# Half of each batch's attention attended a phase later, one stage a slot, with the first loads and weights asked for in another order

## The chip, the cores and the metric

The kernel runs on one core of a Trainium2 chip. A core has five engines that run beside each other, each with its own instruction stream: TensorE (PE in the profile; its weight loads are PEld), VectorE (DVE), ScalarE (ACT), GpSimd (POOL) and SyncE (SP, which here only starts DMAs). DMAs that SP starts and DMAs that GpSimd starts stand in different queues of the same 16 DMA engines. The metric is the device time of one execution in microseconds (us); the kernel before took 290.09 us, the median of three runs.

## The reference

Attention over a sliding window of 128 keys with 4 always visible first keys ("sinks"), followed by a gated feed-forward network (FFN). Everything comes in and goes out in float32.

```python
# q, k, v: (4, 8, 768, 64) = batch, heads, positions, head size
scores = matmul(q, k.T) / sqrt(64)
keep = (key < 4) | ((0 <= query - key) & (query - key < 128))
a = softmax(where(keep, scores, -1e9))
attn = matmul(a, v)                                  # (4, 8, 768, 64)
x = attn.transpose(0, 2, 1, 3).reshape(3072, 512)    # heads side by side
out = (maximum(x @ w_gate, 0) * (x @ w_val)) @ w_out # w: 512x1536, 512x1536, 1536x512
```

## The kernel before

**Units.** Two heads of one batch make a unit; there are 16 units, 4 to a batch, U[0] to U[15]. A unit goes through stages, each a function:

- `load_kq` (lines 91 to 93) and `load_v` (95 to 104) start its DMAs on SP: two for keys and queries into `kf` and `qf` (three buffers each), six for values into `vf` (four buffers).
- `cast_kq` (115) and `cast_v` (109, 111) turn them into bf16 on GpSimd: `kn` and `qn` (two buffers each), `vn` (four).
- `T` (line 179) transposes keys and queries on TensorE, 48 small matmuls, and ScalarE copies them out as `kE` and `qT`. In the head (while `head[0]` is true) the query copy is VectorE's.
- `Sg(u, g)` (197 to 207), shortened to S: the scores of group g (0, 1 or 2), on TensorE, and their exp on ScalarE. The band mask is added by two more matmuls (line 197, `bias=True`) for batch 0, and multiplied in by VectorE (line 207) for the others.
- `V(u, part)` (218 to 228): values and row sums of one half of the unit's 768 positions, on TensorE, then four VectorE operations that divide and write into `xT`. Half 0 needs S of groups 0 and 1, half 1 of groups 1 and 2.

**The FFN.** `chunk(b, g, m)` (lines 240 to 247) computes column block m (128 of the 1536 hidden columns, 12 blocks) of half g of batch b: four matmuls with `wg`, four with `wv`, a relu on ScalarE, a product on VectorE. It needs half g of all four units of batch b. `ffn2` (260 to 265) is one matmul with `w_out`; after twelve of them ScalarE copies a block of the output and SP stores it.

**Weights.** `load_w(m0, m1)` (line 123) starts two DMAs on GpSimd's queue, for column blocks m0 to m1 of `wg` and `wv`; `load_wo` (127) does so for a third of `w_out`. These DMAs turn float32 into bf16 on their way.

**Order.** The program is written under a manual schedule: each engine executes its instructions in the order of the text. A head prepares units 0 to 3 and attends the first half of each. Then follow 96 slots, one chunk each; behind the chunk stand the stages that `plan` has put into the slot, and then up to three queued `ffn2` calls (there are some from slot 24 on). Slots 0 to 23 belong to batch 0's FFN, and batch 1 is attended in them: 30 stages, of which the first six go one to a slot and the other 24 into slots 6 to 23 (`plan[6 + x * 18 // 24]`). All of batch 1, both halves, is attended in the first 24 slots, all of batch 2 in the next 24, and so on. From slot 24 on there is one stage a slot, up to slot 71. `pre` puts a unit's preparation, `front`, four slots ahead of its `T`: casts of keys, queries and values, and then the loads of the unit after it.

`gate(u)` (line 119) writes two elements of the key buffer from GpSimd. The load of that buffer, on SP, must wait for this write, and so cannot start before GpSimd has come to this place in its order.

The lines in the profile are those of this listing.

Of the kernel before, what the change touches and what calls it, by code (L numbers as in the profile page):

```python
# [19 lines left out]
def kernel(  # L20
# [12 lines left out]
    nc = tc.nc  # L33
# [54 lines left out]

    U = [Unit(i) for i in range(B * NP)]

    def load_kq(u):
        for x, dst in ((k, kf[u.i % NQ]), (q, qf[u.i % NQ])):
            nc.sync.dma_start(out=dst[:], in_=x[u.b, 2 * u.p:2 * u.p + 2].rearrange("h (p n) d -> (h p) (n d)", n=NR))

    def load_v(u):

# [16 lines left out]
    def cast_kq(u):  # L113
        for src, dst in ((kf[u.i % NQ], kn[u.i % 2]), (qf[u.i % NQ], qn[u.i % 2])):
            nc.gpsimd.tensor_copy(dst[:], src[:])  # L115
# [151 lines left out]
    with tc.manual_schedule():  # L267
        for i in range(NV):
            nc.vector.memset(vf[i][:, 6, :, :], 0.0)
        for i, what in ((0, load_kq), (1, load_kq), (2, load_kq), (0, load_v)):  # L270
            what(U[i])
        setup()
        gp_copy, ve_copy = nc.gpsimd.tensor_copy, nc.vector.tensor_copy
        cast_kq(U[0])
        T(U[0])
        cast_kq(U[1])
        T(U[1])
        load_kq(U[3])
# [32 lines left out]
        def prep(i):  # L311
            cast_kq(U[i])
            cast_v(U[i], gp_copy)

        def load(i):
            if i < len(U):
                load_kq(U[i])
                load_v(U[i])

        def front(i):  # L320

            prep(i)
            if i == 4:
                gate(U[5])
                load(5)
                load_w(8, 12)
            elif i == 5:
                gate(U[6])
                load(6)
# [5 lines left out]
        f2 = deque()  # L335
        slots = [(0, 0, m) for m in range(6)] + [(0, 1, m) for m in range(6)]
        slots += [(0, g, m) for m in range(6, FM) for g in range(2)]
        for b in range(1, B):
            slots += [(b, g, m) for g in range(2) for m in range(FM)]
        plan = [[] for _ in slots]  # L340
        first = [("V", 0, 1), ("S", 2, 2), ("V", 1, 1), ("S", 3, 2), ("V", 2, 1), ("V", 3, 1)]
        for s, x in enumerate(first):
            plan[s].append(x)
        later = [("T", NP, 0)]
        for i in range(NP, len(U)):
            later.append(("S", i, 0))
            if i > NP:
                later.append(("V", i - 1, 1))
            later.append(("S", i, 1))
            if i + 1 < len(U):  # L350
                later.append(("T", i + 1, 0))
            later += [("V", i, 0), ("S", i, 2)]
        later.append(("V", len(U) - 1, 1))
        for x, st in enumerate(later):
            plan[6 + x * 18 // 24 if x < 24 else x].append(st)
        pre = [[] for _ in slots]
        for s, p in enumerate(plan):
            for st in p:
                if st[0] == "T":
                    pre[max(0, s - 4)].append(st[1])  # L360
        for s, (b, g, m) in enumerate(slots):
# [55 lines left out]
```

## Time and profile before

| | |
|---|---|
| three runs | 290.72, 290.09, 287.62 us; median 290.09 |
| profiled execution | 290.54 us, of which its span (first to last instruction) is 288.8 |
| TensorE busy | 264.0 us, 91% of the span |
| VectorE, ScalarE, GpSimd busy | 146.0, 131.3, 59.9 us |
| read from memory | 28.48 MB, 120 GB/s over the span |
| mean granted TensorE clock | 0.969 of full speed |

The profile is of one execution. Times count from the span's start. A row of the timeline has start and length in us, the engine, the line of the kernel, the operation, output and inputs by their names with shapes, and in brackets the idle time before it and what ended it; neighbouring instructions of one line are merged (x8). A small q behind an engine's name (SPq) is its instruction queue, where DMAs are started. TensorE can be given a lower clock for a time; the granted clock says what share of full speed it had. Matmuls are pipelined and their ends are modelled, so start to start of neighbouring rows is a better measure than a row's length.

### The profile page before, as it was taken

To read this page: it belongs to the slowest core of one execution; us is meant where nothing else is said; L and a number is where in the kernel's file an instruction comes from. 1 tells how busy PE (TensorE), PEld (TensorE's weight loads), DVE (VectorE), ACT (ScalarE), POOL (GpSimd) and SP (SyncE) were. 2 spreads that over 40 slices of the span, in tenths; PEclk is the share of its full clock that TensorE was granted. 3 is DMA by queue.
4 is the path that set the end of the run, shared out by engine and by line. 5 is a ranking of instruction groups with operands and counts; after the bars stand their busy time and mean duration, and the time that the engine had idled before them with its cause. 6 is when DMAs were issued, how large, how long until landed. Compare 5 with 4: busy or idle time off the path is not lost.

```text
span 288.8 us, 6483 instructions
## 1 busy us (share of the span) xinstructions
PE 264.0 (91%) x2648; PEld 146.0 (51%) x2648; DVE 146.0 (51%) x287; ACT 131.3 (45%) x262; POOL 59.9 (21%) x87
## 2 busy tenths in 40 slices
PE   2983699598998999999999999999999999999994
PEld 1441365355555455555555555555555555555441
DVE  5373357348778655656564646565567322332100
ACT  3581123564675645464545464654543223233221
POOL 7661551614641302240042104000000000000000
PEclk9997589889999999999999999999999999999999
DMA  7999879599970006430346006010000010010122
GB/s 245 289 161 238 141 156 203 103 221 237 299 193 2 0 2 201 132 75 36 96 125 186 36 7 198 36 39 2 36 37 2 37 39 36 36 39 36 72 79 104
DMA packets 40557, 30.46 MB, mean 105 GB/s; under 512 B 27728, under 2 KB 33360, under 8 KB 40528
## 3 DMA queue, kind: packets, MB, share of 16 engines
q1 hardware_dynamic: 34720, 25.34, 29.7%
q0 software_dynamic: 5808, 4.72, 10.9%
q8 instruction: 20, 0.33, 0.5%
q14 instruction: 9, 0.07, 0.1%
HBM read 28.48 MB, written 6.29 MB: 120 GB/s over the span
## 4 chain that ended last, share of the span: by engine, by line
PE 79%; DVE 8%; DMA 5%; ACT 3%; SPq 2%; issue 1%; POOL 1%; ACTq 0%
PE g L240 20%; PE g L260 20%; PE g L245 20%; PE pp L218 6%; PE pp L201 4%; PE pp L260 4%; PE pp L179 3%; DMA vf<-in_v_dram 3%; DVE R L226 2%; DMA qf<-in_q_dram 2%; DVE t L224 2%; DVE xT L228 1%; PE pp L197 1%; SPq L98 1%; ACT qT L187 1%
## 5 line engine op out<-in xcount | busy, mean ns | idle before, releaser
L247 DVE TENSOR_TENSOR hT<-gs,g 128x384 bf16<-128x384 f32 x96 | 53.0, 552 | 77.4 <-PE g L245 50.9
L243 ACT ACTIVATE gs<-g 128x384 f32<-128x384 f32 x96 | 47.7, 496 | 78.0 <-PE g L240 77.2
L240 PE MATMUL g<-xT,wg 128*128 128x384 bf16 x384 | 80.3, 332 | 3.0 <-DVE xT L228 3.0
L245 PE MATMUL g<-xT,wv 128*128 128x384 bf16 x384 | 79.5, 331 | 0.0
L260 PE MATMUL g<-wo,hT 128*128 128x512 bf16 x240 | 64.4, 382 | 0.0
L205 ACT ACTIVATE ee<-pp 128x998 bf16<-128x998 f32 (+2 forms) x48 | 46.0, 966 | 34.2 <-PE pp L201 34.0
L240 PEld LDWEIGHTS <-wg 128*128 128x128 bf16 x384 | 35.9, 98 | 33.2 <-issue 2.9
L245 PEld LDWEIGHTS <-wv 128*128 128x128 bf16 x384 | 37.9, 99 | 28.2 <-issue 4.0
L260 PEld LDWEIGHTS <-hT 128*128 128x128 bf16 x288 | 24.2, 98 | 25.2 <-issue 3.3
L207 DVE TENSOR_TENSOR ee<-ee,msk 128x998 bf16<-128x998 bf16 (+2 forms) x36 | 24.9, 691 | 22.2 <-ACT ee L205 22.2
L115 POOL CAST kn<-kf 128x768 bf16<-128x768 f32 x16 | 14.1, 878 | 75.2 <-DMA kf<-in_k_dram 65.6
L201 PE MATMUL pp<-qT,kE 64*128 64x255 bf16 (+4 forms) x224 | 19.0, 262 | 3.9 <-DVE xT L228 2.0
L109 POOL CAST vn<-vf 128x896 bf16<-128x896 f32 x16 | 15.1, 946 | 35.5 <-DMA vf<-in_v_dram 26.8
L218 PEld LDWEIGHTS <-vn 128*64 128x64 bf16 x288 | 12.8, 113 | 17.9 <-issue 9.3
L264 ACT COPY ot<-g 128x512 f32<-128x512 f32 x20 | 11.9, 594 | 17.4 <-PE g L260 17.4
L226 DVE STREAM_TRANSPOSE R<-r 128x384 f32<-128x384 f32 x32 | 18.5, 578 | 1.1
L201 PEld LDWEIGHTS <-kE 64*128 64x128 bf16 x224 | 7.4, 96 | 21.1 <-issue 17.9
L224 DVE STREAM_TRANSPOSE t<-pp 128x384 f32<-128x384 f32 x28 | 16.2, 580 | 3.5 <-PE pp L218 3.2
L228 DVE TENSOR_TENSOR xT<-pp,R 128x384 bf16<-128x384 f32 x28 | 15.6, 557 | 1.0
L115 POOL CAST qn<-qf 128x768 bf16<-128x768 f32 x16 | 13.6, 853 | 8.3 <-DMA qf<-in_q_dram 8.2
L218 PE MATMUL pp<-ee,vn 128*64 128x255 bf16 (+8 forms) x256 | 14.8, 242 | 0.0
L218 PE MATMUL pp<-ee,ones 128*64 128x255 bf16 (+8 forms) x256 | 14.0, 237 | 0.0
(54 smaller groups left out, 151.0 us busy)
## 6 DMA issues: line engine op xcount, KB each, us to landing
kf<-in_k_dram SPq DMA_DIRECT2D x16, 384.0 KB, 3.3
qf<-in_q_dram SPq DMA_DIRECT2D x16, 384.0 KB, 4.2
out_dram<-ot SPq DMA_DIRECT2D x24, 256.0 KB, 2.0
vf<-in_v_dram SPq DMA_DIRECT2D x48, 64.0 KB, 4.5
vf<-in_v_dram SPq DMA_DIRECT2D x32, 96.0 KB, 3.6
wo<-in_moe_w_out_dram POOLq DMA_DIRECT2D x3, 512.0 KB, 10.5
wg<-in_moe_w_gate_dram POOLq DMA_DIRECT2D x2, 512.0 KB, 6.5
wv<-in_moe_w_val_dram POOLq DMA_DIRECT2D x2, 512.0 KB, 8.7
```

What stands on the lines that cost most here:

```text
L115: nc.gpsimd.tensor_copy(dst[:], src[:])
L201: nc.tensor.matmul(out=ps[:, h, c0:c1], lhsT=kE[t][64 * h:64 * h + 64, x0:x0 + 128], rhs=qT[t][64 * h:64 * h + 64, q0:q0 + c1 - c0], start ...
L205: nc.scalar.activation(x, ps[:, :, 0:n], Act.Exp, bias=0.0, scale=scale)
L207: nc.vector.tensor_tensor(x, x, msk[:, g, 0:n].unsqueeze(1).to_broadcast([128, 2, n]), op=Alu.mult)
L218: nc.tensor.matmul(out=(pv, pd)[which][64 * h:64 * h + 64, o0:o0 + c1 - c0], lhsT=w, rhs=ee[u.i % NE][:, g, h, c0:c1], start=i == 0, stop= ...
L224: nc.vector.transpose(out=t1[:], in_=pd[:, 0:CUT])
L226: nc.vector.transpose(out=R[:].rearrange("p (c e) -> p c e", e=32), in_=r[:].unsqueeze(2).to_broadcast([128, CUT // 32, 32]))
L240: nc.tensor.matmul(out=gp[:, 0:CUT], lhsT=wg[:, ko, m * 128:(m + 1) * 128], rhs=x[:, ko, c], start=ko == 0, stop=ko == KO - 1)
L243: nc.scalar.activation(gs[:], gp[:, 0:CUT], Act.Relu, bias=0.0, scale=1.0)
L245: nc.tensor.matmul(out=vp[:, 0:CUT], lhsT=wv[:, ko, m * 128:(m + 1) * 128], rhs=x[:, ko, c], start=ko == 0, stop=ko == KO - 1)
L247: nc.vector.tensor_tensor(h[:, m, c], gs[:], vp[:, 0:CUT], op=Alu.mult)
L260: nc.tensor.matmul(out=op, lhsT=hT[b % 2][:, m, t * 128:(t + 1) * 128], rhs=wo[:, m, :], start=m == 0, stop=m == FM - 1)
```

## The change

It has three parts. The first key and query loads (units 0 to 2) are started on ScalarE's queue instead of SP's. The first weights are asked for later in GpSimd's order: two column blocks at a time, the first behind unit 2's value cast, two more behind unit 3's, and two pairs at the end of the head, with unit 4's loads between them; unit 4's loads stood ahead of unit 3's value cast and now stand behind it. And the stages are put into slots from a written order: one stage a slot (but for slot 6, which has two), where the second half of a batch's units, S of group 2 and V of half 1, is attended among the first halves of the next batch. Batch 0's chunks go in other steps (eight blocks of each half, then four of each). Key and query casts and value casts get slots of their own, and every load has its gate. `f2`'s part of the loop and everything not shown is as it was.

```diff
-    def load_kq(u):
+    def load_kq(u, eng=nc.sync):
         for x, dst in ((k, kf[u.i % NQ]), (q, qf[u.i % NQ])):
-            nc.sync.dma_start(out=dst[:], in_=...)
+            eng.dma_start(out=dst[:], in_=...)
...
-        for i, what in ((0, load_kq), (1, load_kq), (2, load_kq), (0, load_v)):
-            what(U[i])
+        for u in U[0:3]:
+            load_kq(u, nc.scalar)
+        load_v(U[0])
         setup()
         gp_copy, ve_copy = nc.gpsimd.tensor_copy, nc.vector.tensor_copy
         cast_kq(U[0])
         T(U[0])
-        cast_kq(U[1])
-        T(U[1])
         load_kq(U[3])
         for u in U[1:4]:
             load_v(u)
+        cast_kq(U[1])
+        T(U[1])
         Sg(U[0], 0, bias=True)
...
         Sg(U[1], 1, bias=True)
-        load_w(0, 2)
         V(U[0], 0)
         cast_v(U[1], ve_copy)
         T(U[3])
-        load_w(2, 4)
         Sg(U[2], 0, bias=True)
         Sg(U[2], 1, bias=True)
         V(U[1], 0)
         cast_v(U[2], ve_copy)
-        gate(U[4])
-        load_kq(U[4])
-        load_v(U[4])
+        load_w(0, 2)
         Sg(U[3], 0, bias=True)
         Sg(U[3], 1, bias=True)
         V(U[2], 0)
         cast_v(U[3], ve_copy)
-        load_w(4, 8)
+        load_w(2, 4)
         Sg(U[0], 2, bias=True)
         V(U[3], 0)
-        Sg(U[1], 2, bias=True)
         head[0] = False
+        load_w(4, 6)

         def load(i):
             if i < len(U):
+                gate(U[i])
                 load_kq(U[i])
                 load_v(U[i])

-        def front(i):
-            prep(i)
-            if i == 4:
-                gate(U[5]); load(5); load_w(8, 12)
-            elif i == 5:
-                gate(U[6]); load(6)
-                for c in range(3):
-                    load_wo(c)
-            else:
-                load(i + 1)
+        load(4)
+        load_w(6, 8)
...
-        slots = [(0, 0, m) for m in range(6)] + [(0, 1, m) for m in range(6)]
-        slots += [(0, g, m) for m in range(6, FM) for g in range(2)]
+        slots = [(0, g, m) for g in range(2) for m in range(8)] + [(0, g, m) for g in range(2) for m in range(8, FM)]
         for b in range(1, B):
             slots += [(b, g, m) for g in range(2) for m in range(FM)]
+        order = [("V", 0, 1)]
+        for i in range(1, NP):
+            order += [("S", i, 2), ("V", i, 1)]
+        x = NP
+        order += [("T", x, 0), ("T", x + 1, 0), ("S", x, 0), ("S", x, 1), ("T", x + 2, 0), ("V", x, 0),
+                  ("S", x + 1, 0), ("S", x + 1, 1), ("T", x + 3, 0), ("V", x + 1, 0), ("S", x + 2, 0),
+                  ("S", x + 2, 1), ("S", x + 3, 0), ("V", x + 2, 0), ("S", x + 3, 1), ("S", x, 2),
+                  ("V", x + 3, 0)]
+        for b in range(2, B):
+            p, n = (b - 1) * NP, b * NP
+            for w in ("Tn0 Vp01 Sp12 Sn00 Vp11 Sp22 Sn01 Vp21 Sp32 Tn1 Vp31 Vn00 "
+                      "Sn10 Sn11 Tn2 Vn10 Sn20 Sn21 Tn3 Vn20 Sn30 Sn31 Sn02 Vn30").split():
+                order.append((w[0], (p if w[1] == "p" else n) + int(w[2]), int(w[3]) if len(w) > 3 else 0))
+        for i in range(len(U) - NP, len(U)):
+            if i > len(U) - NP:
+                order.append(("S", i, 2))
+            order.append(("V", i, 1))
         plan = [[] for _ in slots]
+        at = {}
+        for x, (what, i, g) in enumerate(order):
+            s = x if x < NP + 3 else x - 1
+            plan[s].append((what, i, g))
+            at[what, i, g] = s
+        prep = [[] for _ in slots]
+        for i in range(NP, len(U)):
+            prep[max(at["T", i, 0] - 4, at.get(("T", i - 2, 0), -1) + 1)].append(("kq", i))
+            prep[max(at["V", i, 0] - 4, at["V", i - NP, 1] + 1)].append(("v", i))
...
         for s, (b, g, m) in enumerate(slots):
-            for i in pre[s]:
-                front(i)
+            for what, i in prep[s]:
+                if what == "kq":
+                    cast_kq(U[i])
+                    load(i + 1)
+                else:
+                    cast_v(U[i], gp_copy)
+            if s == 4:
+                load_w(8, 12)
+            if s == 9:
+                for c in range(3):
+                    load_wo(c)
             chunk(b, g, m)
```

Of the stages of the old plan (`first`, and `later` with its steps of 18 slots for 24 stages) all are in the new order; the work of the stages is the same.

More of the change, by code (lines that the diff above doesn't have):

```diff
@@ L304 @@
         cast_v(U[3], ve_copy)
-        load_w(4, 8)
+        load_w(2, 4)
         Sg(U[0], 2, bias=True)
         V(U[3], 0)
-        Sg(U[1], 2, bias=True)
         head[0] = False
-        def prep(i):
-            cast_kq(U[i])
-            cast_v(U[i], gp_copy)
+        load_w(4, 6)
         def load(i):
             if i < len(U):
+                gate(U[i])
                 load_kq(U[i])
                 load_v(U[i])
-        def front(i):
-            prep(i)
-            if i == 4:
-                gate(U[5])
-                load(5)
+        load(4)
@@ new lines @@
+        load_w(6, 8)
+        slots = [(0, g, m) for g in range(2) for m in range(8)] + [(0, g, m) for g in range(2) for m in range(8, FM)]
+        for b in range(1, B):
+            slots += [(b, g, m) for g in range(2) for m in range(FM)]
+        order = [("V", 0, 1)]
[6 more added lines that the diff above has]
+                  ("V", x + 3, 0)]
@@ new lines @@
+        plan = [[] for _ in slots]
+        at = {}
[7 more added lines that the diff above has]
+            prep[max(at["V", i, 0] - 4, at["V", i - NP, 1] + 1)].append(("v", i))
+        f2 = deque()
+        for s, (b, g, m) in enumerate(slots):
+            for what, i in prep[s]:
[5 more added lines that the diff above has]
+            if s == 4:
@@ L326, in front @@
                 load_w(8, 12)
-            elif i == 5:
-                gate(U[6])
-                load(6)
+            if s == 9:
                 for c in range(3):
                     load_wo(c)
-            else:
-                load(i + 1)
-        f2 = deque()
-        slots = [(0, 0, m) for m in range(6)] + [(0, 1, m) for m in range(6)]
-        slots += [(0, g, m) for m in range(6, FM) for g in range(2)]
-        for b in range(1, B):
-            slots += [(b, g, m) for g in range(2) for m in range(FM)]
@@ L340 @@
[L340 to L361, printed above, removed]
-            for i in pre[s]:
-                front(i)
             chunk(b, g, m)
```

2 lines of the change are left out of this document (1 added, 1 removed).

## The prediction

> **What bounds the kernel now.** I read the page's slices first, then a table of stretches, then the chain of waits, and last the timelines of the queues in the stage that has holes. The page's slices (digits are tenths busy or tenths of full clock, 7.2 us a slice):
>
> ```profile
> span 288.8 us, 6483 instructions
> PE   2983699598998999999999999999999999999994
> PEclk9997589889999999999999999999999999999999
> DMA  7999879599970006430346006010000010010122
> ```
>
> From the fourteenth slice TensorE never falls below 9. The holes and the low clock lie in the first third, where the DMA engines are near full. The stretches (length, busy time of PE, PEld, DVE, ACT, POOL, then granted clock, DMA share, GB/s):
>
> ```profile
> 20.58:34.13 13.55, 5.56 (x49) 2.96 (x49) 5.12 (x11) 2.79 (x4) 4.91 (x7) 0.67 0.98 188
> 34.13:96.77 62.64, 56.18 (x709) 33.30 (x708) 39.50 (x77) 31.79 (x68) 24.20 (x33) 0.94 0.77 169
> 96.77:288.80 192.03, 187.95 (x1624) 101.99 (x1620) 90.03 (x168) 84.48 (x163) 16.22 (x20) 1.00 0.20 65
> 20.00:25.00 5.00, 0.86 (x8) 0.23 (x6) 1.25 (x3) 1.68 (x2) 0.96 (x2) 1.00 1.37 207
> 50.00:55.40 5.40, 1.85 (x53) 1.22 (x52) 2.10 (x5) 2.27 (x7) 3.65 (x6) 1.00 0.37 80
> 55.40:59.00 3.60, 3.58 (x17) 1.36 (x18) 1.14 (x2) 1.49 (x2) 0.82 (x1) 0.56 1.03 179
> ```
>
> Slots 0 to 23 run from the first FFN chunk at 34.13 to 96.77, slot 24 to the end from 96.77. The head's end, 20.58 to 34.13, waits for values:
>
> ```profile
> 30.40 1.00 PE L218 MATMUL g<-ee,vn 128*64 128x247 bf16 x8 [2.82 <-POOL vn L109]
> ...
> 34.13 1.44 PE L240 MATMUL g<-xT,wg 128*128 128x384 bf16 x4 [0.86 <-DVE xT L228]
> ```
>
> **What a slot costs TensorE.** Pieces of the chain of waits, each the time until the next piece (start, us):
>
> ```profile
> 42.01 0.83 PE pp L218 x20
> 42.84 0.76 PE g L240 x4
> 43.60 0.65 PE g L245 x4
> 44.25 0.35 PE pp L197 x2
> 44.60 0.29 PE pp L201 x6
> ...
> 52.67 0.89 PE pp L179 x48
> ...
> 73.35 0.72 PE pp L218 x16
> ```
>
> A chunk is 0.76 + 0.65 = 1.41 us, V of a second half 0.83, V of a first half 0.72, T 0.89, S 0.29, S with mask bias 0.35 + 0.29 = 0.64. Slots 0 to 23 of before hold 24 chunks (33.8), 7 second-half V (5.8), 4 first-half V (2.9), 5 T (4.5), 12 S (3.5) and 2 biased S (1.3): 51.8 us of work in 62.64, so 10.8 us are stalls and half clock.
>
> **Part by part.**
>
> *Slots.* The order written by the change puts in slots 0 to 23: 24 chunks (33.8), 4 second-half V (3.3), 4 first-half V (2.9), 5 T (4.5), 9 S (2.6), 3 biased S (1.9): 49.0 us. Three second-half V and three S go behind slot 24 (3 x 0.83 + 3 x 0.29 = 3.4), where nothing hides them: 192.0 + 3.4 = 195.4 us from slot 24 to the end. One biased S comes from the head into slot 1; it is counted. So moving alone saves no TensorE work; what is to be won is the 10.8 us and the head.
>
> *Head: loads, weights, clock.* POOL and SP rows:
>
> ```profile
> 16.73 0.96 POOL L109 CAST vn<-vf 128x896 bf16<-128x896 f32 x1
> ...
> 29.42 0.93 POOL L109 CAST vn<-vf 128x896 bf16<-128x896 f32 x1 [4.73 <-DMA vf<-in_v_dram]
> 30.29 0.74 POOL L123 DMA_DIRECT2D wg<-in_moe_w_gate_dram  x1
> 31.02 0.76 POOL L123 DMA_DIRECT2D wv<-in_moe_w_val_dram  x1
> ```
>
> ```profile
> 13.75 0.35 SPq L104 DMA_DIRECT2D vf<-in_v_dram  x1
> 14.14 2.47 SPq L98 DMA_DIRECT2D vf<-in_v_dram  x5
> ...
> 17.11 5.54 SPq L98 DMA_DIRECT2D vf<-in_v_dram  x5
> ...
> 39.28 0.34 SPq L93 DMA_DIRECT2D kf<-in_k_dram  x1
> ...
> 52.73 0.34 SPq L93 DMA_DIRECT2D kf<-in_k_dram  x1
> ...
> 60.33 0.63 SPq L93 DMA_DIRECT2D kf<-in_k_dram  x1
> ```
>
> Unit 1's values, with no weights yet on the way, were cast 16.73 - 13.75 = 3.0 us after their last issue. Unit 2's first five issues took 2.47 us and the sixth 0.35; unit 3's five, issued while weights moved, took 5.54. At unit 2's pace they end at 17.11 + 2.9 = 20.1 (an estimate from these rows), and the cast comes 3.0 later, at 23.1 instead of 29.42. Before, the first chunk followed that cast by 34.13 - 29.42 = 4.7 us at half clock; at full clock I take 3.9: first chunk at 27.0, 7.1 earlier. On POOL the weights' issues now stand behind casts that wait for values: the first two column blocks (128 columns of w_gate and of w_val each) behind unit 2's cast, the next two pairs of blocks behind unit 3's. It is the first chunk that waits for them; the list of DMA issues gives the time from issue to landing of such a block pair's half beside other traffic:
>
> ```profile
> wv<-in_moe_w_val_dram POOLq DMA_DIRECT2D x2, 256.0 KB, 8.9
> ```
>
> Unit 2's last value issue ends at 17.1, its cast runs at 20.1 to 21.0, so this half is asked for at 21.8 (0.74 us for the other half first); it lands at 30.7 by this row; at the other end, with no values on the way, it lands inside the 3.9. I take the early end, since both queues have only weights left by then, and keep 30.7 for a rival. The six first loads on ScalarE's queue cost it six issues of 0.34 to 0.63 us (the L93 rows), covered: it has only its table load and a warm-up to do before the first T. If that cover were gone, 2.0 to 3.8 us would fall on the first T's copies. The trace has no ScalarE load, so what it does to the landings is bounded by those issue times on either side: values up to 2.8 us earlier, or keys and queries as much later. The DMA share at the head is near full whoever asks, so I take 0. Writing unit 3's loads and the values ahead of the second cast and T moves no instruction on its own engine: nothing.
>
> *The load chain becomes the pace.* In the changed kernel load i+1 waits for unit i's key and query casts, for every unit (gate; before for units 4 to 6). The ends of such links, units 5 to 8:
>
> ```profile
> 45.91 0.82 POOL L115 CAST qn<-qf 128x768 bf16<-128x768 f32 x1 [2.74 <-DMA qf<-in_q_dram]
> ...
> 60.80 0.82 POOL L115 CAST qn<-qf 128x768 bf16<-128x768 f32 x1 [3.84 <-DMA qf<-in_q_dram]
> ...
> 71.32 0.82 POOL L115 CAST qn<-qf 128x768 bf16<-128x768 f32 x1
> ...
> 75.23 0.82 POOL L115 CAST qn<-qf 128x768 bf16<-128x768 f32 x1 [0.43 <-DMA qf<-in_q_dram]
> ```
>
> ```profile
> 70.75 0.34 SPq L93 DMA_DIRECT2D kf<-in_k_dram  x1
> ```
>
> From key issue to end of the query cast: 7.4, 8.9 and 11.8 us beside weights (units 5 to 7), 5.3 (70.75 to 76.05, unit 8) without. In the changed kernel load(4) stands behind unit 3's cast (24.0), four weight issues (4 x 0.75) and the gate: 27.1. Column blocks 4 to 11 and then w_out fill the software queue behind it, so I price the four links to unit 7 at the mean of the contested three, 9.4: 36.5, 45.9, 55.3, 64.7. T of units 4, 5, 6, 7 stands in slots 6, 7, 10, 14. A T may start half its length, 0.4 us, before its link ends, since the key half goes first. TensorE comes to T(4) after six slots (3 x 2.24 + 3 x 2.05 = 12.9) and a chunk and V (2.2), at 27.0 + 15.1 = 42.1: no stall. It comes to T(5) at 42.1 + 0.9 + 1.4 = 44.4: stall 1.1, to 45.5. To T(6), past T(5), two slots with S and a chunk (0.9 + 3.4 + 1.4), at 51.2: stall 3.7, to 54.9. To T(7), past T(6), a slot with V, two with S and a chunk (0.9 + 2.1 + 3.4 + 1.4), at 62.7: stall 1.6, to 64.3. So the head's gain is handed back in part: without these 6.4 us the slots would run as counted, and a first chunk that is later by up to 6.4 us costs nothing. The value casts, now in slots of their own (7, 11, 15, 18 for units 4 to 7), stand behind the key casts on POOL; their V come at 11, 15, 19, 22, at least a slot behind the T that POOL waits with, so I take nothing for them. If they were late, it would be by their own contested landing, as unit 3's above.
>
> Behind T(7) stand T itself 0.9, slots 15 to 22 with 8 chunks, 5 S and 3 first-half V (14.9), slot 23 with T(8) (2.3): 18.1; and 195.4: together 213.5. In 195.4 I count no stall: the stretch 96.77:288.80 of before, also one stage a slot, has PE busy 187.95 of 192.03 at full clock, and each S keeps at least one slot between itself and its V.
>
> *Clock.* After the two waits in 50.00:55.40 the clock was 0.56 for 3.6 us, a loss of 1.6. Cooling at T(6) is swallowed by T(7)'s wait; after T(7) it counts. Bounds 0 and 1.6, I take 0.8. The Trainium skill (TensorE: Matmul & The Clock Gate, Part 1) lets the clock fall only after an idle window of about 3.4 us. By that rule the T(7) term would be 0 and the sum 0.8 smaller; the trace agrees in 20.00:25.00 (busy 0.86 of 5.00, and then a mean of 0.67), and is hard to square with it in 50.00:55.40, where 1.85 us of work lie between the waits.
>
> *Sum.* 64.3 + 213.5 + 0.8 = 278.6 us of span. The profiled execution took 290.54 for its span of 288.8, so 1.7 lies around it; it stands 0.4 above the runs' median of 290.09. Forecast: 278.6 + 1.7 - 0.4 = 279.9 us.
>
> **Rivals.** *No stall in the slots* (the loads come in time): then T(7) starts at 27.0 + 30.9 (slots 0 to 14 up to it) = 57.9, and 57.9 + 213.5 + 1.3 = 272.7 us. For it: a link without weights takes 5.3 us, so four from 27.1 would end at 48.3; against: weights are asked for through the whole stretch, and all three contested links took over 7.
>
> *The software queue goes first*, ending slower. The queues' totals on the page, then in the windows 60 to 66 and 56 to 58 (packets, MB, share of 16 engines):
>
> ```profile
> q0 software_dynamic: 5808, 4.72, 10.9%
> ```
>
> ```profile
> q0 software_dynamic: 929, 0.93, 91.1%
> q1 hardware_dynamic: 923, 0.24, 29.6%
> ```
>
> ```profile
> q0 software_dynamic: 316, 0.32, 107.6%
> q1 hardware_dynamic: 4, 0.01, 1.7%
> ```
>
> The 4.72 MB are twelve pairs of column blocks (0.26 MB a pair) and w_out (1.57). In the last window the loads on SP's queue got almost nothing beside 0.16 MB/us of weights. If every link waits for the weights ahead of it, eight blocks (2.1 MB, 13.1 us from the second issue's end at 22.6) end at 35.7; link 4 (5.3) and link 5 (5.3) follow, then blocks 8 to 11 (1.05 MB, 6.6) and link 6 (5.3), then w_out (9.8) and link 7 (5.3): 73.3. With a value load (2.9) ahead of each of links 5 to 7 it is 82.0. T(7) starts 0.4 earlier, and 213.5 + 0.8 + 1.3 more make 289 to 297 us; I take 294. It is slower than before once T(7) starts after 74.5, and by over 1% after 77.4. Against it: 929 packets to 923 in the first window. The Trainium skill (DMA: Bandwidth & Descriptors, Queues, rings and completion order) has each engine take the queues in turn, packet by packet. By that rule the 2 us of the second window would not be lost, the 8.9 us link would be 6.9, the mean 8.7, and the sum 2.7 us smaller; the first window agrees, the second does not.
>
> *The head isn't shortened*: weights land last, first chunk at 30.7 or later. Then TensorE, with the stalls at T(5) and T(6) smaller by as much, still comes to T(7) before 64.3, and the forecast stands; only from 33.4 on does each us cost one, and at the old 34.13 it would be 280.6. The price is so small because the loads would end last either way; it is part of the first case.
>
> **How the numbers follow.** Load-paced as forecast 0.60 (links from 8 to 11 us: 274 to 286); no stall 0.22; software queue first 0.13, half of it slower by over 1%; the rest 0.05, about no change. About 1% is what a measurement of this kernel can tell from none. Faster 0.82, same 0.11, slower 0.07. The range goes from the no-stall case, with the first chunk up to 2.7 us earlier than I took it, to the start of the queue case: 270 to 288.
>
> **What would show it.** Unit 3's cast near 23 and the first chunk near 27 (head); slots 0 to 23 at 27 to 83 with stalls named by POOL's casts at T(6) and T(7) (load chain); slot 24 to the end 3 us longer than 192.0 (moved work). Wrong, if T(7) has no wait for kn or qn, if the first chunk waits for wg or wv beyond 34, or if slots after 24 show PE idle.

## The result, and the profile after

The changed kernel takes 279.02 us, the median of four runs (278.06 to 281.48), against 289.49 us (four runs, 287.62 to 290.72) for the kernel before on the same chip. The ratio is 0.9657, with a 95% interval of 0.9573 to 0.9741: faster by 3.4%. Forecast were 279.9 us, range 270 to 288. The profiled execution is the slowest of the four, 281.48 us, with a span of 279.8. In this section and below, executions that came out slower than the rest of their kernel's at a lower granted clock are left out of the ratios, but not of the medians.

The page of the changed kernel, the same slices as before (now 7.0 us each):

```profile
span 279.8 us, 6462 instructions
PE   1796699995999999999999999999999999999994
PEclk9999599999999999999999999999999999999999
DMA  7957997999620157157101257100101000010122
```

From the head's end on two slices are still below 9: the fifth (28 to 35 us, in which the head ends), with a low clock, and the tenth. The stretches (columns as in the prediction's table: length, busy PE, PEld, DVE, ACT, POOL, then clock, DMA share, GB/s):

```profile
30.30:34.40 4.10, 4.10 (x28) 2.25 (x27) 0.55 (x1) 0.49 (x1) 0.00 (x0) 0.51 1.24 229
34.40:62.50 28.10, 28.10 (x373) 16.77 (x370) 18.16 (x36) 16.95 (x38) 10.10 (x16) 1.00 1.10 228
30.30:84.37 54.07, 51.24 (x639) 29.94 (x638) 33.35 (x65) 28.70 (x60) 19.23 (x31) 0.96 0.95 202
84.37:279.80 195.43, 189.21 (x1676) 104.57 (x1698) 96.71 (x180) 87.29 (x171) 21.55 (x33) 1.00 0.22 70
```

The first chunk starts at 30.30 (before 34.13), slots 0 to 23 take 54.07 us (before 62.64), and the rest 195.43 (before 192.03). So 3.8 us were won in the head and 8.6 in the slots, and 3.4 were given back behind them. Within the slots there are only two losses: the first 4.1 us at half clock, and a wait at `T` of unit 7. From 34.40 to 62.50 TensorE is busy all the time. TensorE's timeline at the two places:

```profile
25.55 0.30 PE L218 MATMUL g<-ee,vn 128*64 128x247 bf16 x2 [0.41 <-POOL vn L109]
27.22 0.37 PE L218 MATMUL g<-ee,vn 128*64 128x252 bf16 x6 [1.37 <-DVE vn L111]
27.44 0.71 PE L218 MATMUL g<-ee,ones 128*64 128x247 bf16 x8
30.30 1.44 PE L240 MATMUL g<-xT,wg 128*128 128x384 bf16 x4 [2.15 <-DVE xT L228]
...
64.96 0.56 PE L179 MATMUL pp<-ident,kn 64*64 64x64 bf16 x24 [1.75 <-POOL kn L115]
66.61 0.56 PE L179 MATMUL pp<-ident,qn 64*64 64x64 bf16 x24 [1.09 <-POOL kf L119]
```

GpSimd's timeline carries both: the head's value casts and weights, and then the ends of the load chain's links.

```profile
19.70 0.92 POOL L123 DMA_DIRECT2D wg<-in_moe_w_gate_dram  x1
...
24.57 0.93 POOL L109 CAST vn<-vf 128x896 bf16<-128x896 f32 x1 [3.19 <-DMA vf<-in_v_dram]
...
36.57 0.82 POOL L115 CAST qn<-qf 128x768 bf16<-128x768 f32 x1 [0.81 <-PE pp L201]
...
44.17 0.82 POOL L115 CAST qn<-qf 128x768 bf16<-128x768 f32 x1 [0.30 <-DMA qf<-in_q_dram]
...
50.95 0.82 POOL L115 CAST qn<-qf 128x768 bf16<-128x768 f32 x1 [1.64 <-DMA qf<-in_q_dram]
...
51.75 2.23 POOL L127 DMA_DIRECT2D wo<-in_moe_w_out_dram  x3
64.08 0.83 POOL L115 CAST kn<-kf 128x768 bf16<-128x768 f32 x1 [10.10 <-DMA kf<-in_k_dram]
65.73 0.83 POOL L115 CAST qn<-qf 128x768 bf16<-128x768 f32 x1 [0.82 <-DMA qf<-in_q_dram]
```

and SP's queue has the starts of those links:

```profile
28.48 0.35 SPq L93 DMA_DIRECT2D kf<-in_k_dram  x1
...
37.45 0.34 SPq L93 DMA_DIRECT2D kf<-in_k_dram  x1
...
45.06 0.34 SPq L93 DMA_DIRECT2D kf<-in_k_dram  x1
...
51.83 0.34 SPq L93 DMA_DIRECT2D kf<-in_k_dram  x1
```

From key issue to end of the query cast (a row's start and length): 37.39 - 28.48 = 8.9 us, then 7.5, 6.7 and 14.7 (66.56 - 51.83). The first three links end before TensorE comes to their `T`; the fourth, beside w_out, ends 3 us late.

### The profile page after: what moved, and what is told of

It is laid out like the page before. It is cut to its first block, busy times and chain, and to the rows that moved or that the text cites. A ratio compares the mean times of both kernels' runs of the same rounds, so it can differ in the third digit from the quotient of the medians.

```text
span 279.8 us, 6462 instructions
## 1 busy us (share of the span) xinstructions
PE 258.2 (92%) x2621; PEld 144.3 (52%) x2648; DVE 146.5 (52%) x287; ACT 130.1 (46%) x262; POOL 60.1 (21%) x98
## 3 DMA queue, kind: packets, MB, share of 16 engines
HBM read 28.48 MB, written 6.29 MB: 124 GB/s over the span
## 4 chain that ended last, share of the span: by engine, by line
PE 78%; DMA 14%; DVE 3%; issue 2%; SPq 1%; POOL 1%; ACT 1%; POOLq 0%; ACTq 0%; DVEq 0%
PE g L240 20%; PE g L260 20%; PE g L245 20%; DMA vf<-in_v_dram 9%; PE pp L218 7%; DMA qf<-in_q_dram 5%; PE pp L201 4%; PE pp L260 4%; PE pp L179 3%; POOL qn L115 1%; PE g L218 1%; DVE t L224 1%; SPq L98 1%; DVE R L226 1%; DVE vn L111 1%
## 5 line engine op out<-in xcount | busy, mean ns | idle before, releaser
L240 PE MATMUL g<-xT,wg 128*128 128x384 bf16 x384 | 79.0, 329 | 2.3 <-DVE xT L228 2.1
L260 PE MATMUL g<-wo,hT 128*128 128x512 bf16 x214 | 60.3, 381 | 2.4 <-issue 1.7
L240 PEld LDWEIGHTS <-wg 128*128 128x128 bf16 x384 | 35.7, 98 | 34.1 <-issue 4.1
L115 POOL CAST kn<-kf 128x768 bf16<-128x768 f32 x16 | 13.2, 826 | 77.8 <-DMA kf<-in_k_dram 77.8
L218 PE MATMUL pp<-ee,vn 128*64 128x115 bf16 (+8 forms) x256 | 14.6, 242 | 0.0
L218 PE MATMUL pp<-ee,ones 128*64 128x115 bf16 (+8 forms) x256 | 14.0, 237 | 0.0
```

Source lines behind the costliest of these rows:

```text
L218: nc.tensor.matmul(out=(pv, pd)[which][64 * h:64 * h + 64, o0:o0 + c1 - c0], lhsT=w, rhs=ee[u.i % NE][:, g, h, c0:c1], start=i == 0, stop= ...
L240: nc.tensor.matmul(out=gp[:, 0:CUT], lhsT=wg[:, ko, m * 128:(m + 1) * 128], rhs=x[:, ko, c], start=ko == 0, stop=ko == KO - 1)
L260: nc.tensor.matmul(out=op, lhsT=hT[b % 2][:, m, t * 128:(t + 1) * 128], rhs=wo[:, m, :], start=m == 0, stop=m == FM - 1)
```

## The experiments

Three questions: what made the fourth link long, what the head lost, and which part of the change brought the 10 us. Each verdict is a ratio to the kernel before, run beside it. The edits are to the changed kernel unless said otherwise.

### w_out asked for seven slots later

```diff
-            if s == 9:
+            if s == 16:
                 for c in range(3):
                     load_wo(c)
```

> Only w_out's three loads move, from slot 9 to slot 16 of GpSimd's order, behind unit 7's key and query casts. Theory A (the software queue's share sets the load chain): unit 7's link, 14.7 us from key issue to the end of the query cast in the changed kernel, falls to 9 to 11, T(7) no longer waits (2.8 us before), and the span goes from 279.8 to 277.0. Theory B (unit 7's loads stand behind unit 6's values in SyncE's own queue, and that sets it): the link stays above 12.5, T(7) waits 1 us or more, span 279 or more. If w_out then comes too late, the first w_out matmul in slot 24 waits, and the span grows by that wait.

Measured: 278.99 us, ratio 0.9655 [0.9594, 0.9717]; profiled execution 278.08, span 276.4. TensorE's timeline at `T` of unit 7:

```profile
62.51 0.57 PE L179 MATMUL pp<-ident,kn 64*64 64x64 bf16 x24
```

The link, issued at 51.57, ends at 60.84: 9.3 us instead of 14.7, and TensorE waits for nothing at `T`. Without w_out beside it the profiled execution has no wait at `T` of unit 7; that w_out alone makes the wait isn't shown, since two runs below have w_out there and no wait either. The w_out matmuls of slot 24 don't wait for the later loads. The median, however, is that of the changed kernel. The changed kernel's profiled execution is its slowest; less the waits of 1.75 and 1.09 its 281.48 would be 278.6, among the other three (278.06, 278.79, 279.25). That points to a wait which most executions don't have, or have smaller; the others have no profile, so this is worked out, not shown.

The list of DMA issues tells how the values fared that stand in SP's queue around unit 7's keys. In the changed kernel, 50 to 64 us:

```profile
vf<-in_v_dram SPq DMA_DIRECT2D x4, 64.0 KB, 9.1
```

and with w_out later, 50 to 62 us:

```profile
vf<-in_v_dram SPq DMA_DIRECT2D x4, 64.0 KB, 3.7
```

In the median a value load of 64 KB took 9.1 us from issue to landing, and 3.7 without w_out beside it.

### w_out first, ahead of column blocks 8 to 11

```diff
             if s == 4:
+                for c in range(3):
+                    load_wo(c)
                 load_w(8, 12)
-            if s == 9:
-                for c in range(3):
-                    load_wo(c)
```

> w_out is asked for at slot 4, ahead of column blocks 8 to 11, so that 1.57 MB more stand on the software queue before unit 6's and unit 7's keys come. Theory A: unit 6's link grows from 6.7 to 10 or more, T(6) waits about 1 us, T(7) 4 to 6 us, span 282. Theory B: the order of the weights makes no difference to the loads, T(7) waits 2 to 3 us, span 280.

Measured: 282.35 us, ratio 0.9683 [0.9597, 0.977]. The profiled execution took 284.38 us; only its order of events is used.

```profile
65.20 0.83 POOL L115 CAST kn<-kf 128x768 bf16<-128x768 f32 x1 [11.75 <-DMA kf<-in_k_dram]
```

With w_out asked for at 45.60, six microseconds earlier, unit 6's link doesn't grow to 10 us as theory A had it (it is 7.7) and its `T` has no wait. It is unit 7's keys and queries again that come late (TensorE waits 3.36 and 0.79 us for them). So it isn't the moment of w_out's issue as such: the weights that are on the way from 46 on fall on the link that begins near 53, behind unit 6's values.

### Values asked for behind the next unit's keys and queries

```diff
         def load(i):
             if i < len(U):
                 gate(U[i])
                 load_kq(U[i])
-                load_v(U[i])
+            if 4 <= i - 1:
+                load_v(U[i - 1])
```

> From unit 4 on a unit's values are asked for behind the next unit's keys and queries instead of ahead of them. Theory B: unit 7's link falls from 14.7 to 8 or less, T(7) does not wait, span 277.0. Theory A: its keys and queries still share with w_out, the link falls by 2 to 3 us at most, T(7) waits up to 1 us, span 278. If both shares are needed, this and the run with w_out late each end at 277.

Measured: 279.10 us, ratio 0.9677 [0.9599, 0.9755]; profiled execution 276.80, span 275.1.

```profile
59.57 0.83 POOL L115 CAST qn<-qf 128x768 bf16<-128x768 f32 x1 [0.81 <-DMA qf<-in_q_dram]
```

Here w_out stands where the change put it (asked for at 51.91), and the fourth link is 60.40 - 51.98 = 8.4 us. `T` of unit 7 has no wait. Without w_out beside it, or without unit 6's values ahead of it, the link is 9.3 and 8.4 us. Both together aren't enough for a long one, though: the next run has both, w_out asked for at 53.22 and the keys at 53.30, and its fourth link takes 9.2 us. The median again is that of the changed kernel.

The trace's packets show where the long link loses its time. Values move in packets of 256 bytes (one row of 64 float32), keys and queries in packets of 3072, w_out in packets of 1024. In each of these runs unit 7's keys first stand behind unit 6's values: in the changed kernel their first packet starts at 55.8, 4.0 us after the issue. Then 230 of the 256 packets of its keys and queries start by 60 us, and the last 26 come one by one among those of w_out and of values, until 65.1. In the next run 247 start by 60 us and the last at 61.1; with w_out late, or with the values behind, all 256 have started by 59.1. So the long link is the last tenth of its packets. Why they lag in one execution and not in another stays open.

### First loads back on SP's queue

```diff
         for u in U[0:3]:
-            load_kq(u, nc.scalar)
+            load_kq(u)
```

> The first key and query loads go back to SyncE's queue; everything else as changed. Theory of the prediction: nothing at the end, within 0.7 us of 279.8 in the span, because what the head gains or loses is swallowed by T(7)'s wait of 2.8 us. Rival: the second queue is a gain of its own: the first chunk comes 2 us later or more than at 30.3, T(7)'s link ends 2 us later, span 282.

Measured: 278.19 us, ratio 0.9613 [0.9544, 0.9681]; span 276.8. ScalarE's first rows with this edit:

```profile
0.81 1.28 ACT L132 ACT_TABLE_LOAD   x1 [0.81 <-PEq L396]
...
5.84 0.26 ACT L183 COPY kE<-g 128x120 bf16<-128x120 bf16 x1 [3.54 <-PE g L179]
```

and in the changed kernel, where ScalarE starts these six loads:

```profile
1.76 0.45 ACTq L93 DMA_DIRECT2D kf<-in_k_dram  x1
4.13 0.33 ACTq L93 DMA_DIRECT2D qf<-in_q_dram  x1
...
7.55 0.33 ACTq L93 DMA_DIRECT2D qf<-in_q_dram  x1
7.91 1.28 ACT L132 ACT_TABLE_LOAD   x1 [7.91 <-DMA vf<-in_v_dram]
...
9.32 0.24 ACT L183 COPY kE<-g 128x120 bf16<-128x120 bf16 x1
```

On ScalarE the six issues last until 7.88, not for six times 0.45 us: the third ends at 2.21 and the fourth starts at 4.13. The table load stands behind them, and the first copy of unit 0 comes 3.5 us later than with the loads on SP. Yet the first chunk is at 29.80 with the edit and at 30.30 without: unit 3's value cast, at 24.32 against 24.57, ends the head either way. The two ratios can't be told apart by their intervals. The expectation, a span within 0.7 us of 279.8, missed: 276.8, because the wait at `T` of unit 7 that was to swallow the difference isn't in this execution.

### The new head alone, and the new order alone

First the kernel before with the changed head only (the loads' queue, the order of weights and of unit 4's loads), its old slots left:

```diff
+        for u in U[0:3]:
+            load_kq(u, nc.scalar)
...
-        load_w(0, 2)
         V(U[0], 0)
...
-        gate(U[4])
-        load_kq(U[4])
-        load_v(U[4])
+        load_w(0, 2)
...
-        load_w(4, 8)
+        load_w(2, 4)
+        load_w(4, 6)
+        gate(U[4])
+        load_kq(U[4])
+        load_v(U[4])
+        load_w(6, 8)
```

> The kernel before with the changed head alone (first loads on ScalarE's queue; weights asked for behind the values of units 2 and 3, unit 4's loads behind blocks 4 and 5), its stages in the old order. Theory (the order of the stages carries most of it): the first chunk comes near 30 instead of 34.13, but the old order keeps most of its 10.8 us of stalls: span 284 to 287, a ratio of 0.985 to 0.995. Rival (the head carries it): span below 282.

Measured: 287.39 us, ratio 0.9973 [0.9937, 1.0009]: no change that can be told, less than the 0.985 to 0.995 expected. Its slots 0 to 23:

```profile
29.62:93.70 64.08, 56.74 (x709) 33.56 (x708) 40.32 (x77) 31.75 (x67) 27.01 (x35) 0.93 0.87 186
```

The first chunk is 4.5 us earlier than before, at 29.62, but the old slots take 64.08 us, 1.4 more than before, and keep their own stalls. Two of them, in TensorE's timeline:

```profile
47.67 0.32 PE L240 MATMUL g<-xT,wg 128*128 128x384 bf16 x1 [1.74 <-DVE xT L228]
...
51.40 0.39 PE L201 MATMUL pp<-qT,kE 64*128 64x247 bf16 x4 [1.88 <-ACT kE L188]
```

Neither is a wait for a load: they are a stage's own chain on VectorE and ScalarE, with too little other work of TensorE between. (S of group 2 of unit 1 stays in this head; in the changed kernel it stands in slot 1.) Then the changed kernel with the old head, its new order of slots kept:

```diff
-            load_kq(u, nc.scalar)
+            load_kq(u)
...
+        load_w(0, 2)
         V(U[0], 0)
...
+        load_w(2, 4)
...
-        load_w(0, 2)
+        gate(U[4])
+        load_kq(U[4])
+        load_v(U[4])
...
-        load_w(2, 4)
+        load_w(4, 8)
...
-        load_w(4, 6)
-        load(4)
-        load_w(6, 8)
```

> The changed kernel with the old head alone. Theory: first chunk near 34 at half clock as before, no wait at T(4) to T(7) because their loads now have 4 us more; slot 24 comes 49 us and 2 to 3 us of half clock behind the first chunk, span 34.1 + 51.5 + 195.4 = 281, a ratio of 0.972. Rival (the head carries it): span 286 or more.

Measured: 281.93 us, ratio 0.9757 [0.9702, 0.9812]; span 281.0.

```profile
33.73:85.60 51.87, 51.87 (x638) 30.18 (x638) 32.98 (x65) 28.70 (x60) 17.84 (x28) 0.94 0.85 182
```

The order alone brings 2.4% (about 7 us; by the interval 1.9 to 3.0%), the whole change 3.4%. In these slots TensorE is busy for all of 51.87 us; what is over the 49.0 counted in the prediction is clock (it was 0.50 until 39.68). The two parts aren't a plain sum: the earlier head is worth nothing that can be measured before the old slots and 2 to 3 us before the new (281.93 us against the 279.74 of the changed kernel again, below, on the same chip; ratios 0.9757 and 0.9661, whose intervals just overlap).

### Three mends at once

```diff
-            load_kq(u, nc.scalar)
+            load_kq(u)
...
-        load_w(0, 2)
         Sg(U[3], 0, bias=True)
         Sg(U[3], 1, bias=True)
         V(U[2], 0)
         cast_v(U[3], ve_copy)
+        load_w(0, 2)
         load_w(2, 4)
...
-            if s == 9:
+            if s == 16:
```

> The changed kernel with first loads back on SyncE's queue, blocks 0 and 1 asked for behind unit 3's value cast, and w_out in slot 16. Theory: unit 3's values meet no weights, its cast comes at 22 to 23 instead of 24.57, the first chunk at 28 instead of 30.3, T(7) does not wait: slot 24 near 79, span 275. Rival (the weights of the first chunk now come last): first chunk at 30 or later, span 277 or more.

Measured: 279.33 us, ratio 0.9671 [0.9619, 0.9722]; span 278.7. GpSimd's and TensorE's rows:

```profile
24.39 0.94 POOL L109 CAST vn<-vf 128x896 bf16<-128x896 f32 x1 [2.07 <-DVE r L225]
```

```profile
29.36 0.89 PE L240 MATMUL g<-xT,wg 128*128 128x384 bf16 x4 [2.64 <-DMA wg<-in_moe_w_gate_dram]
31.38 1.46 PE L245 MATMUL g<-xT,wv 128*128 128x384 bf16 x4 [1.13 <-DMA wv<-in_moe_w_val_dram]
```

With no weights ahead of it, unit 3's cast is at 24.39, where it was (24.57 and 24.32 above), so the theory fell. This doesn't show that the weights of blocks 0 and 1 cost the last values nothing, since the run also moved the first loads. With these on SP's queue SP starts the last of unit 3's values at 22.52 (22.53 in the run that moved them alone), in the changed kernel at 20.95. From there to the cast it takes 1.9 us here, 1.8 in that run, where the weights come only from 22.21 on, and 3.6 in the changed kernel, where they come from 19.70 on. The earlier start and the slower landing cancel; that it is the weights that slow the landing is likely by these rows, not shown. And the weights now come last, as the rival had it: the chunk, at 29.36, waits for `wg` and then 1.13 us more for `wv`.

### The changed kernel again

> The changed kernel as it is, beside the three others on one chip. If T(7)'s wait of 2.8 us is in every execution, it stays 2 us or more behind the run with w_out late (which had 278.99 us median); if the wait comes and goes with the exact time at which w_out is asked for, its median stays within 1 us of that, and its slowest executions are the ones with the wait.

The same kernel, six runs: 279.74 us, ratio 0.9661 [0.9604, 0.9719]. Five of the executions lie between 277.17 and 279.89. The profile shows the wait at `T` of unit 7 again (1.12 and 1.21 us), but fell on the sixth and slowest, of 282.96, as the first profile had fallen on the slowest. The median is within 1 us of 278.99, as expected of a wait that comes and goes; whether the faster executions are without it stays open.

### TensorE kept at work in the head's last waits

```diff
+    def fill(n):
+        ps = PP[(rot[0] + 1) % 2]
+        for _ in range(n):
+            nc.tensor.matmul(out=ps[:, 0, 0:507], lhsT=ident[:], rhs=msk[:, 1, 0:507], start=True, stop=True)
...
+        fill(6)
         V(U[3], 0)
+        fill(9)
...
-            if s == 9:
+            if s == 16:
```

> The changed kernel with w_out asked for in slot 16 (as in the run that moved w_out alone, median 278.99 us) and with idle work for TensorE in the two last waits of the head: six matmuls of 128x507 on the mask ahead of unit 3's first V, nine behind it, their results unused. Theory (half clock): the remaining loss of the head is the granted clock, which falls in the waits of 0.41, 1.37 and 2.15 us and costs 2.2 us in slot 0; with the waits filled the first slots run at full clock in every execution, the first chunk comes within 0.3 us of 29.8, two chunks and the V between them end 2.2 us earlier than at half clock, T(7) has no wait, and the median falls by 1 to 2 us, to 277 to 278. Rival (the pace behind the head is set by loads): the first slots run at full clock, but the gain is lost in a wait of T(4) to T(7) for POOL's casts, and the median stays at 279. Rival (filler in the way): the fifteen matmuls delay unit 3's V and the first chunk by 0.5 to 1 us, and the median is 279 to 280.

Measured: 277.07 us, ratio 0.9588 [0.9558, 0.9618]; span 276.4. The granted clock is 0.998 to 1.000 in all six runs; in the four runs of the changed kernel it was 0.986 to 0.988, and in its six runs again 0.982 to 0.994, so its loss isn't the same in every execution. First the slots of the run that moved w_out alone, then the slots with the filler:

```profile
29.79:80.97 51.18, 50.91 (x639) 29.86 (x638) 34.06 (x65) 28.80 (x60) 20.28 (x32) 0.96 1.00 214
```

```profile
31.95:81.04 49.09, 49.09 (x638) 29.05 (x637) 33.66 (x65) 28.70 (x60) 19.81 (x31) 1.00 0.96 210
```

The same 24 slots take 51.18 us, their first 3.7 at half clock, and 49.09 at full clock. Of the 2.1 us between them 0.27 are idle time of TensorE (50.91 busy), so about 1.8 us are the price of the clock here. That is near what was expected; the first chunk isn't: in this execution it came at 31.95, because unit 2's first V was late already (24.77, against 22.88 in the changed kernel), ahead of the filler. Full clock made up for those 2.2 us, and slot 24 starts at 81.04 against 80.97. By the medians the filler is worth 1.9 us (277.07 against 278.99, on different chips; ratios 0.9588 and 0.9655, whose intervals overlap a little).

### All of it in one kernel

The filler, w_out in slot 16, the first loads on SP's queue, values behind the next keys, and unit 3's sink rows copied by GpSimd:

```diff
-        cast_v(U[3], ve_copy)
+        cast_v(U[3], gp_copy)
```

> All that the runs before point to in one kernel: first loads on SP's queue, w_out in slot 16, from unit 4 on values asked for behind the next unit's keys and queries, unit 3's sink rows copied by GpSimd right behind its cast instead of by VectorE behind V(2)'s chain, and the idle work for TensorE of the run beside this one. Theory (the costs lie in different places and add): first chunk at 28.4 (unit 3's rows 1.4 us earlier), full clock, no wait at T(4) to T(7), so slot 24 at 28.4 + 49.0 = 77.4 to 79, and 195.4 behind it: span 273 to 274.5, median 274 to 276. Rival (one hides the other): with a first chunk this early the links of 8 to 10 us end at 36, 44, 52 and 61 while TensorE comes to T(7) at 59, T(7) waits 1 to 2 us again for the query half, and the median is 277 to 278.

Measured: 276.44 us (274.72 to 277.66, six runs), ratio 0.9556 [0.9519, 0.9593]: faster than the kernel before by 4.4%, and the fastest kernel here. Span 274.6. Its slots 0 to 23:

```profile
28.58:79.11 50.53, 49.33 (x638) 29.20 (x637) 35.09 (x65) 28.81 (x60) 22.04 (x33) 1.00 1.01 214
```

First chunk at 28.58 and slot 24 at 79.11, close to what the theory expected. The span is 0.1 and the median 0.4 above its ranges: with TensorE earlier, short waits return (0.62 us for a query half, 0.59 for VectorE's product). Against the filler run alone (0.9588) the gain can't be told.

## Why the prediction was right, and where its steps were not

The total was right, 279.9 forecast and 279.02 measured, and the profiled execution's span was 279.8 where the sum said 278.6. The mechanism was right in the main (work moved without loss, a head that ends earlier, a load chain that TensorE meets at the end), but that the total came out so close is in part luck. That TensorE meets the chain's end is seen in the profiled executions of this kernel, the slowest ones; whether the faster ones meet it isn't shown, and where they don't, the head, the clock and the work set their time. Point by point:

**The moved work: right.** The prediction counted 49.0 us of TensorE work in slots 0 to 23 and 195.4 from slot 24 on. The run at full clock without waits has 49.09, and the last stretch is 195.3 to 195.4 in every kernel with the new order. (Of the old 30 stages in these slots six finish batch 0 and one is `T` of unit 8; V of half 1 of unit 7 stood in slot 25, so not quite all of batch 1 was attended there. The counts above have this right.) The 10.8 us of stalls and half clock of the old slots were the prize, as said, and the run with the old head shows that the order wins most of it.

**The load chain: the sum right, the terms not.** Four links of 9.4 from 27.1 to 64.7 were forecast, 37.6 us; measured are 38.1, from 28.48 to 66.56. But the links are 8.9, 7.5, 6.7 and 14.7. The step that failed is the mean of before's three contested links applied to all four: with column blocks 4 to 11 beside them the first three were 7.7 in the mean, and the fourth stood behind unit 6's values and beside w_out. The mean itself had a link in it that isn't only a load. The 11.8 us of unit 7 end behind the cast of unit 6's values; GpSimd's rows of the kernel before:

```profile
69.10 0.93 POOL L109 CAST vn<-vf 128x896 bf16<-128x896 f32 x1 [7.47 <-DMA vf<-in_v_dram]
70.55 0.82 POOL L115 CAST kn<-kf 128x768 bf16<-128x768 f32 x1
```

The key cast waits for no DMA of its own, it waits its turn behind the value cast, and the new order puts that cast behind unit 7's. The other two links, 7.4 and 8.9, have a mean of 8.2. So the stalls of 1.1 at T(5) and 3.7 at T(6) didn't occur at all, also because TensorE came to them 5.1 and 4.1 us later than forecast (49.55 and 55.28 against 44.4 and 51.2), and the wait at T(7) was 2.8 instead of 1.6.

**The head: mis-sized.** Unit 3's cast came at 24.57 instead of 23.1: the issues of its values ended 1.2 us later than the 20.1 estimated, and their landing, beside weights, took 3.3 us more instead of 3.0. The chunk followed the cast by 5.7 us instead of 3.9: the copy of the sink rows stood on VectorE behind unit 2's V (TensorE's wait of 1.37), and from 27.5 on the clock was half. The chunk started 3.3 us later than forecast. "A first chunk that is later by up to 6.4 us costs nothing" held in part: the profiled execution came to T(7) before its link ended, so there the head cost nothing, but where the link isn't long, the head sets the time, and the last two runs gained there.

**The clock: wrong place.** 0.8 us were put behind T(7), where none was lost (from 66.2, where T(7) would start in one piece, the remainder is 213.6, against 213.5 without that term). About 1.9 us were lost in slot 0, which the prediction ran at full clock: its chunk and V take 4.11 us from start to start, and 2.22 with the filler. In the profiled execution 30.3 + 49.1 + 1.9 + 2.8 = 84.1 come near the start of slot 24 at 84.37, where the forecast had 27.0 + 49.0 + 6.4 + 0.8 = 83.2. Too early a head and too many stalls nearly cancelled, and that is luck.

**ScalarE's loads: the cover wasn't there.** "It has only its table load and a warm-up to do before the first T" is true, but the issues lasted until 7.88, and T of unit 0 starts at 4.95. The bound of 2.0 to 3.8 us on T's copies was right (3.5 us). It cost the end little, since the values end the head.

**The rivals.** No stall in the slots (272.7): its picture, TensorE busy from the first chunk to T(7), holds in the profiled runs that moved w_out alone, the values alone or the first loads alone, but with a first chunk 2 to 3 us later and half clock behind it their medians are 278.2 to 279.1, not 272.7. The head isn't shortened: fell for the changed kernel, whose first chunk waits for VectorE's `xT` and not for weights; a first chunk that waits for weights is what the run with three mends had (at 29.36). Software queue first (294): fell as a price for every link, but the behaviour is there. In the window 60 to 66 us of the changed kernel, beside w_out, the two queues had

```profile
q0 software_dynamic: 925, 0.91, 89.7%
q1 hardware_dynamic: 922, 0.30, 31.7%
```

one packet for one. This agrees with the rule of the Trainium skill (DMA: Bandwidth & Descriptors, Queues, rings and completion order), that each engine takes the queues in turn by packets. By that rule the links were to be 8.7: the first three are 7.7 in the mean, the fourth 14.7. But stretches like the 316 to 4 of before came again. In the changed kernel no packet of SP's queue started from 30 to 32 us, though unit 4's keys had been asked for at 28.48; in the last kernel, from 46 to 48, it was 3, while unit 6's queries, asked for at 43.45, were awaited:

```profile
q0 software_dynamic: 589, 0.29, 128.1%
```

```profile
q0 software_dynamic: 366, 0.37, 119.0%
q1 hardware_dynamic: 3, 0.01, 0.8%
```

What makes these stretches isn't known. The window 60 to 66 shows how a link's end can be slow without them. A packet of the software queue carried 0.91/925 MB there, about 1 KB, and one of SP's a third of it in the mean (most were value packets of 256 bytes), so taken turn by turn w_out got three quarters of the bytes.

## What to carry to other kernels

A head and an order of stages must be judged together: the earlier head was worth nothing before slots that stalled on their own chains, and 2 to 3 us before slots that didn't. Price each link of a load chain by what is on the other queue at that moment, not by a mean, and keep large weight loads out of the links that someone waits for. When an old link is taken as a price, look whether its end waited for a load or for an engine's turn. Where TensorE waits several times within a few microseconds ahead of dense work, look at the granted clock of the work behind it as well as at the waits; idle matmuls in the waits can pay.

## What the runs showed of the hardware that was not expected

**Half clock after short waits.** In the changed kernel the clock was down by the row at 27.44 (0.71 us for eight matmuls that take 0.46 at full clock), after waits of 0.41 and 1.37 us with 0.3 us of work between them, and it stayed down until 34.33, 4.0 us into dense work. The kernel before with the new head had it after a wait of 1.56 us, 0.2 us into the next: its first L240 row is 1.44 us long, against 0.81 at full clock.

The Trainium skill (TensorE: Matmul & The Clock Gate, Part 1) has the clock fall after an idle window of about 3.4 us. No single wait in these two was that long, so by that rule read as one stretch of idleness the clock would have stayed up, and the measurement decides against it. The length agrees with the traces, which show steps of 3.41 us. In all twelve profiles each stretch at half clock that begins between 20 and 70 us lasts 3.41, 6.82 or 13.65 us, one, two or four steps, and where an execution has two of them, their starts lie 7, 9 or 11 steps apart. So the clock seems to be set once a step, by how busy TensorE was in it, and the same waits can cost or not by where the steps fall. In the first profile of the changed kernel the clock fell at 27.50. In the profile of its repeat, with waits of 0.43 and 1.37 us in the same place, it stayed up until 28.98 (the first row below is the changed kernel's; then two of the repeat; the last is the kernel before):

```profile
27.50:34.33 6.83, 4.68 (x42) 2.80 (x36) 2.50 (x5) 0.49 (x1) 2.43 (x5) 0.50 1.30 208
```

```profile
25.57:28.98 3.41, 0.71 (x16) 0.66 (x15) 2.45 (x6) 0.22 (x1) 3.41 (x7) 1.00 0.83 99
28.98:35.80 6.82, 6.00 (x34) 3.14 (x34) 2.95 (x7) 0.88 (x2) 1.51 (x2) 0.50 1.25 236
```

```profile
48.99:52.41 3.42, 1.68 (x20) 0.94 (x14) 2.55 (x6) 0.35 (x1) 1.18 (x2) 1.00 0.36 75
```

In the step before a fall TensorE was busy for 0.09 to 0.54 of it. Yet in the kernel before a step at 0.49 (the last row) left the clock up. So the limit isn't settled here. With waits of 0.47 and 0.54 us, the filler between them, the clock stayed at 1.00.

**DMA issues that hold an engine.** ScalarE's fourth load started 1.9 us after its third had been issued, with nothing on ScalarE in between, and the table load's idle time is put down to a value load of SP's queue (the row at 7.91 above). Whatever such issues wait for, here the computation of the engine that issues them waited behind it (the table load at 7.91, against 0.81 with these loads on SP). SP has no computation that could wait.
